# Feeding an FFN's weights through the sync queue in fp32 with casts on the engines, and refitting the instruction order

## The chip, the cores and the metric

One core of a Trainium2 chip. The metric is the device time of one execution in microseconds (us). One execution of each kernel was also recorded by the hardware profiler; its span is 1 to 2 us shorter than its time. Engines: PE is TensorE, DVE VectorE, ACT ScalarE, POOL GpSimd, SP the sync engine, which only issues DMAs here. All runs told below were in the fast state (mean granted TensorE clock 0.986 or more in every profile) and all were correct, unless said.

## The reference

A gated recurrence over time for 256 channels, and a multiplicative feed-forward net on its output; all in fp32, 4 sequences of 5824 tokens.

```python
a_base = sigmoid(a_param)
a   = exp(8 * sigmoid(r_gate) * log(clip(a_base, 1e-6, 1 - 1e-6)))
xg  = sqrt(max(1 - a*a, 1e-6)) * sigmoid(i_gate) * x
h   = 0
for t in range(S):                       # the scan
    h = a[:, t] * h + xg[:, t]; y[:, t] = h
out = ((y @ w1) * (y @ w2)) @ w3 @ w_out # w1, w2: 256x1024, w3: 1024x1024, w_out: 1024x256
```

## The kernel before

The 23,296 tokens are cut into 46 chunks: one of 256 tokens, then 45 of 512. For each chunk ScalarE takes the tanh of the gates (th_r, th_i), th_r and u = (1 + tanh) x are transposed, ScalarE makes the decay a_t (exp) and the square root (nrm), VectorE multiplies and scans (h_t), a cast gives y_t in bf16. TensorE then makes two "up" products, pa (on w1) and pb (on w2); ScalarE copies pa to sa, VectorE multiplies sa and pb to g_t, and TensorE makes the "down" product po. In the trace a table load of 1.28 us stands wherever ScalarE changes between exp or tanh and sqrt (30 in all, with the one at the start), so several chunks share one pair of table loads: such a set is a *group*.

w3 and w_out are multiplied once at the start (the *fold*), wp = w3 @ w_out / 4, so that each chunk needs only one down product. For this TensorE transposes w3 (ptw), VectorE copies it (w3t), TensorE multiplies (pw), and pw is copied to wp.

No instruction order is written down. A scheduler in Python takes jobs, each with an engine, a duration and a due time, plays them through, and issues them in the order it finds. That order is then fixed on every engine. The due times are offsets found by search:

```python
group_sizes = [2, 2, 1, 3, 3, 3, 4, 4, 4, 4, 4, 4, 4, 4]
NPE = 8      # chunks below this are transposed on TensorE, later ones by DMA
NDV = 3      # chunks below this have u and the squares on VectorE, later ones on GpSimd
NCV = 4      # chunks below this have y_t cast on VectorE
LAG = 17.5   # how long after a chunk's ups its downs are due
D_LOAD, D_TANH, D_EXP, D_SQRT, D_GATE, D_SCAN, D_CAST = 16.0, 9.0, 13.5, -1.5, 11.0, 8.5, 2.5
SPREAD = 9.9
...
def load_w(mp, w_sb, w_in):              # fp32 in HBM, bf16 on chip: cast by the DMA
    cols = slice(2 * mp * P, 2 * (mp + 1) * P)
    nc.gpsimd.dma_start(out=w_sb[:, :, cols], in_=w_in.rearrange("(cb p) f -> p cb f", p=P)[:, :, cols])

def load_wo():
    nc.gpsimd.dma_start(out=wo_sb, in_=moe_w_out.rearrange("(ko p) f -> p ko f", p=P))

def load_w3(mi):
    T["w3", mi] = consts.tile([P, DFF], BF16, name="w3_t", tag="w3_%d" % mi)
    nc.gpsimd.dma_start(out=T["w3", mi], in_=moe_w3[mi * P:(mi + 1) * P, :])
...
def fold_e(mi):
    nc.vector.tensor_scalar(wp_sb[:, mi, :], T["pw", mi], 0.25, None, op0=ALU.mult)
...
job((nm, mp), "POOL", 0.8, DUE_W + mp, partial(load_w, mp, w_sb, w_in), mb=0.26)   # w1, w2: four pieces each
```

## Time and profile before

| before | us |
|---|---|
| time, median of 3 (lowest to highest) | 540.92 (540.48 to 541.2) |
| x of chunk 1 has landed | 14.9 |
| first matmul of an up product | 20.86 |
| first down product (the fold is complete) | 70.65 |
| first ScalarE copy of chunk 4 / of chunk 12 / of chunk 45 | 83.7 / 175.0 / 521.4 |
| span | 540.3 |

The copies are good milestones: each chunk has exactly four (sa), and a copy cannot start before its up product is done. "Chunk 4" below means the start of its first copy. The page's busy shares and stretches are read in the prediction. Two more lines matter later, those of the DMA queues (columns: packets, MB, share of the 16 DMA engines' time):

```profile
q1 hardware_dynamic: 177104, 115.37, 80.6%
q0 software_dynamic: 4368, 3.67, 4.2%
```

q1 is the sync queue with everything else, q0 the GpSimd queue with the weights. The weights are under 5% of the DMA time; what they cost is when they run, not how long.

### The profile page before, as it was taken

The page shows a single profiled execution, that of the slowest core. Times are in us where ns is not written, and L with a number is a line of the kernel's source. Part 1 is how long each engine was busy: PE and PEld are TensorE (multiplying, and loading weights), DVE is VectorE, ACT ScalarE, POOL GpSimd, SP SyncE. Part 2 cuts the span into 40 slices and gives each one's busy share as a digit, 9 for nine tenths or more (in the row PEclk, how much of TensorE's full clock was granted, in tenths as well). Part 3 has the DMA queues.
Part 4 walks back from the last instruction along what each step waited for, and adds up shares of the span by engine and source line. Part 5 has one row for each costly group of instructions (what it writes and reads, how often), then busy time and mean ns, then how long its engine had stood idle before and what let it go on. Part 6 is the DMA issues. An engine that isn't in the chain of part 4 may idle for free.

```text
span 540.3 us, 8712 instructions
## 1 busy us (share of the span) xinstructions
PE 504.2 (93%) x3176; PEld 306.9 (57%) x3176; DVE 435.2 (81%) x360; ACT 458.3 (85%) x537; POOL 351.3 (65%) x280
## 2 busy tenths in 40 slices
PE   1577999999979999999999999999999999999996
PEld 1344676655545555665656556546565656556555
DVE  1867679868888699888999899889897998999541
ACT  6792799998997999999998899998999997854553
POOL 4083468885969678878884877978787869331000
PEclk9996999999998999999999999999999999999999
DMA  9999458999997999999899999999899943311112
GB/s 218 323 330 241 115 169 264 285 281 245 272 273 190 252 302 269 276 265 282 258 270 250 284 239 240 285 303 241 267 241 260 288 123 75 97 41 41 59 39 98
DMA packets 181788, 119.61 MB, mean 221 GB/s; under 512 B 84464, under 2 KB 180720, under 8 KB 181744
## 3 DMA queue, kind: packets, MB, share of 16 engines
q1 hardware_dynamic: 177104, 115.37, 80.6%
q0 software_dynamic: 4368, 3.67, 4.2%
q8 instruction: 25, 0.41, 0.3%
q14 instruction: 19, 0.16, 0.1%
q10 hardware_dynamic: 272, 0.00, 0.0%
HBM read 78.91 MB, written 23.86 MB: 190 GB/s over the span
## 4 chain that ended last, share of the span: by engine, by line
PE 73%; issue 7%; DVE 7%; ACT 6%; DMA 4%; POOL 2%; SPq 0%; DVEq 0%; ACTq 0%; POOLq 0%
PE po L242 24%; PE pa L221 24%; PE pb L221 23%; DVE g_t L235 3%; ACT sa L228 3%; DMA x_t<-in_x_dram 2%; DVE h_t L205 2%; DMA w_t<-in_moe_w_dram 2%; PE pw L280 1%; ACT nrm L185 1%; DVE nrm L190 1%; POOL u_t L145 1%; ACT a_t L173 1%; ACT ot L248 1%; ACT th_r L120 1%
## 5 line engine op out<-in xcount | busy, mean ns | idle before, releaser
L235 DVE TENSOR_TENSOR g_t<-sa,pb 128x1024 bf16<-128x1024 bf16 (+1 forms) x184 | 218.6, 1198 | 60.8 <-ACT sa L228 50.0
L221 PEld LDWEIGHTS <-w_sb 128*128 128x128 bf16 x1472 | 145.0, 99 | 162.0 <-issue 16.0
L228 ACT CAST sa<-pa 128x1024 bf16<-128x1024 f32 (+1 forms) x184 | 183.4, 1000 | 49.8 <-PE pa L221 45.5
L221 PE MATMUL pa<-y_t,w_sb 128*128 128x512 bf16 (+1 forms) x736 | 190.4, 382 | 12.3 <-DVE y_t L213 6.2
L221 PE MATMUL pb<-y_t,w_sb 128*128 128x512 bf16 (+1 forms) x736 | 189.4, 380 | 1.7 <-ACT sa L228 1.4
L242 PE MATMUL po<-wp_sb,g_t 128*128 128x256 bf16 x1456 | 179.7, 273 | 0.1
L242 PEld LDWEIGHTS <-g_t 128*128 128x128 bf16 x1456 | 142.7, 98 | 43.1 <-issue 0.7
L205 DVE TENSOR_TENSOR_SCAN h_t<-a_t,h_t,nrm 128x512 f32<-128x512 f32 (+3 forms) x90 | 140.1, 1567 | 2.0
L147 POOL TENSOR_TENSOR u_t<-th_i,x_t 128x512 bf16<-128x512 f32 x76 | 122.4, 1628 | 2.5
L181 POOL TENSOR_TENSOR nrm<-a_t 128x512 f32<-128x512 f32 x86 | 106.4, 1251 | 18.3 <-ACT a_t L173 18.2
L213 POOL CAST y_t<-h_t 128x1024 bf16<-128x1024 f32 x42 | 52.8, 1258 | 100.3 <-DVE h_t L205 85.5
L248 ACT COPY ot<-po 128x512 f32<-128x512 f32 x91 | 53.3, 586 | 19.6 <-PE po L242 19.0
L132 POOL TENSOR_SCALAR th_i<-th_i 128x1024 f32<-128x1024 f32 x43 | 48.0, 1117 | 27.0 <-ACT th_i L127 26.6
L190 DVE SCALAR_TENSOR_TENSOR nrm<-nrm,ut 128x1024 f32<-128x1024 f32 x38 | 56.7, 1492 | 8.7 <-ACT nrm L185 7.6
L173 ACT ACTIVATE a_t<-rt,la 128x512 f32<-128x512 bf16 x76 | 60.6, 819 | 0.2
L127 ACT ACTIVATE th_i<-i_t 128x1024 f32<-128x1024 f32 (+1 forms) x46 | 48.3, 1051 | 1.1 <-DMA i_t<-in_i_gate_dram 1.0
L185 ACT ACTIVATE nrm<-nrm 128x1024 f32<-128x1024 f32 (+1 forms) x46 | 48.0, 1056 | 1.4 <-DVE nrm L181 1.2
L120 ACT ACTIVATE th_r<-r_t 128x1024 bf16<-128x1024 f32 x38 | 40.3, 1062 | 0.4 <-DMA r_t<-in_r_gate_dram 0.4
L185 ACT ACT_TABLE_LOAD x14 | 18.0, 1283 | 0.2
L155 PE MATMUL ptr<-ident,th_r 128*128 128x128 bf16 x60 | 5.7, 249 | 10.6 <-DVE ident L73 8.7
L173 ACT ACT_TABLE_LOAD x11 | 14.1, 1283 | 0.7 <-DVE la L288 0.5
L145 POOL TENSOR_TENSOR u_t<-th_i,x_t 128x512 bf16<-128x512 f32 x10 | 13.5, 1360 | 0.3
(33 smaller groups left out, 112.0 us busy)
## 6 DMA issues: line engine op xcount, KB each, us to landing
out_dram<-ot SPq DMA_DIRECT2D x91, 256.0 KB, 3.1
r_t<-in_r_gate_dram SPq DMA_DIRECT2D x45, 512.0 KB, 5.4
i_t<-in_i_gate_dram SPq DMA_DIRECT2D x45, 512.0 KB, 5.5
x_t<-in_x_dram SPq DMA_DIRECT2D x45, 512.0 KB, 5.4
w_t<-in_moe_w_dram POOLq DMA_DIRECT2D x8, 256.0 KB, 10.8
w_sb<-in_moe_w_dram POOLq DMA_DIRECT2D x8, 128.0 KB, 9.3
rt<-th_r SPq DMA_TRANSPOSE x38, 4.2
ut<-u_t SPq DMA_TRANSPOSE x38, 4.3
```

The source lines that it names most:

```text
L147: nc.gpsimd.tensor_mul(out=u.rearrange("p cb j q -> p j cb q")[:, js], in0=cut(t)[:, js], in1=cut(T["x", c])[:, js])
L173: nc.scalar.activation(out=T["a", c][:, cb, :w], in_=T["pr", c][:, cb, :w], func=AF.Exp, scale=la4[:, cb:cb + 1], bias=la4[:, cb:cb + 1])
L181: eng.tensor_mul(out=T["n", c][:, cb, :w], in0=T["a", c][:, cb, :w], in1=T["a", c][:, cb, :w])
L185: nc.scalar.activation(out=T["n", c][:, :, :w], in_=T["n", c][:, :, :w], func=AF.Sqrt, scale=-1.0, bias=1.0)
L190: nc.vector.scalar_tensor_tensor(out=T["n", c][:, :, :w], in0=T["n", c][:, :, :w], scalar=1e-3, in1=T["pu", c][:, :, :w], op0=ALU.max, op1 ...
L205: nc.vector.tensor_tensor_scan(T["h", c][:, cb, lo:hi], T["a", c][:, cb, lo:hi], T["n", c][:, cb, lo:hi], init, ALU.mult, ALU.add)
L213: eng.tensor_copy(out=T["y", c][:, :, :w], in_=T["h", c][:, :, :w])
L221: nc.tensor.matmul(out=pp[:, q, :w], lhsT=w_sb[:, cb, m * P:(m + 1) * P], rhs=T["y", c][:, cb, :w], start=(cb == 0), stop=(cb == NCB - 1))
L228: nc.scalar.copy(out=sa[:, :, :w], in_=T["pa", c, mp][:, :, :w])
L235: nc.vector.tensor_mul(out=T["g", c][:, 2 * mp:2 * mp + 2, :w], in0=T["sa", c, mp][:, :, :w], in1=T["pb", c, mp][:, :, :w])
L242: nc.tensor.matmul(out=T["po", c, j // 2][:, j % 2, :], lhsT=T["g", c][:, k, j * P:(j + 1) * P], rhs=wp_sb[:, k, :], start=(k == 0), stop= ...
L248: nc.scalar.copy(out=T["ot", c, j2], in_=T["po", c, j2])
```

## The change

The intent: keep the weights from competing with the first chunks' data, by putting them into the sync queue's fixed order; pay for it with cast instructions on engines that idle at the start; and fit the scheduler's numbers again around that. It is two changes in one, a new path for the weights and a new order of everything. The core of the diff (parts that are switched off, renamings, and the due times of the weights and the fold are cut):

```diff
-    group_sizes = [2, 2, 1, 3, 3, 3, 4, 4, 4, 4, 4, 4, 4, 4]
+    group_sizes = [2, 2, 2, 3, 3, 4, 4, 4, 4, 3, 4, 2, 5, 4]
-    NPE = 8
-    NDV = 3
-    NCV = 4
+    NPE = 6
+    NDV = 4
+    NCV = 8
+    NWF = 2
+    FEA = True
+    WCE = {'w1': 'POOL', 'w2': 'POOL', 'wo': 'POOL', 'w3': 'DVE'}
-    LAG = 17.5
-    D_LOAD, D_TANH, D_EXP, D_SQRT, D_GATE, D_SCAN, D_CAST = 16.0, 9.0, 13.5, -1.5, 11.0, 8.5, 2.5
-    SPREAD = 9.9
+    DUE_WH = 8.0
+    LAG = 21.5
+    D_LOAD, D_TANH, D_EXP, D_SQRT, D_GATE, D_SCAN, D_CAST = 18.0, -13.5, 10.0, -0.5, 15.0, 10.0, 5.0
+    SPREAD = 4.9
...
-    def load_w(mp, w_sb, w_in):
-        cols = slice(2 * mp * P, 2 * (mp + 1) * P)
-        nc.gpsimd.dma_start(out=w_sb[:, :, cols], in_=...)
+    def load_w(key, piece):                      # 512 KB in fp32, into one of two staging buffers
+        T[key] = held.tile([P, NCB, CT], F32, name="wf", tag="wf", bufs=NWF)
+        nc.sync.dma_start(out=T[key]..., in_=piece)
+
+    def cast_w(key, dst, eng):
+        ...
+        if eng == "ACT":
+            nc.scalar.copy(out=dst, in_=t)
+        else:
+            (nc.gpsimd if eng == "POOL" else nc.vector).tensor_copy(out=dst, in_=t)
...
     def fold_e(mi):
-        nc.vector.tensor_scalar(wp_sb[:, mi, :], T["pw", mi], 0.25, None, op0=ALU.mult)
+        if FEA:
+            nc.scalar.mul(wp_sb[:, mi, :], T["pw", mi], 0.25)
...
-    SLOT = 10.3
+    SLOT = 10.1
-    RATE = 0.285
+    RATE = 0.33
```

w1 and w2 come in two halves each, w_out in two, w3 in eight rows of blocks: 14 loads, 14 casts (six on GpSimd, eight on VectorE).

More of the change, by code (lines that the diff above doesn't have):

```diff
@@ L86 @@
     AHEAD = 2
-    NPE = 8
-    NDV = 3
-    NCV = 4
+    NPE = 6
+    NDV = 4
+    NCV = 8
     NHELD = 6
-    BACKLOG = 0.5
-    DUE_W = -13.0
-    DUE_W3 = 14.0
-    DUE_F = 27.0
-    LAG = 17.5
-    D_LOAD, D_TANH, D_EXP, D_SQRT, D_GATE, D_SCAN, D_CAST = 16.0, 9.0, 13.5, -1.5, 11.0, 8.5, 2.5
-    SPREAD = 9.9
+    NWF = 2
+    FTD = False
+    FCA = False
+    FEA = True
+    WCE = {'w1': 'POOL', 'w2': 'POOL', 'wo': 'POOL', 'w3': 'DVE'}
+    BACKLOG = 0.5
+    DUE_W = -4.0
+    DUE_W3 = 20.5
+    DUE_WH = 8.0
+    DUE_F = 25.5
+    LAG = 21.5
+    D_LOAD, D_TANH, D_EXP, D_SQRT, D_GATE, D_SCAN, D_CAST = 18.0, -13.5, 10.0, -0.5, 15.0, 10.0, 5.0
+    SPREAD = 4.9
     src = {"r": rf, "i": jf, "x": xf}
@@ L253, in store @@
                           in_=T["ot", c, j2])
-    def load_w(mp, w_sb, w_in):
-        cols = slice(2 * mp * P, 2 * (mp + 1) * P)
-        nc.gpsimd.dma_start(out=w_sb[:, :, cols], in_=w_in.rearrange("(cb p) f -> p cb f", p=P)[:, :, cols])
-    def load_wo():
-        nc.gpsimd.dma_start(out=wo_sb, in_=moe_w_out.rearrange("(ko p) f -> p ko f", p=P))
-    def load_w3(mi):
-        T["w3", mi] = consts.tile([P, DFF], BF16, name="w3_t", tag="w3_%d" % mi)
-        nc.gpsimd.dma_start(out=T["w3", mi], in_=moe_w3[mi * P:(mi + 1) * P, :])
+    def load_w(key, piece):
+        T[key] = held.tile([P, NCB, CT], F32, name="wf", tag="wf", bufs=NWF)
+        nc.sync.dma_start(out=T[key] if len(piece.shape) == 3 and piece.shape[1] == NCB else
+                          T[key].rearrange("p a b -> p (a b)").rearrange("p (k f) -> p k f", f=piece.shape[-1]),
+                          in_=piece)
+    def cast_w(key, dst, eng):
+        t = T[key]
+        if dst is None:
+            T["w3b", key[1]] = dst = ffn.tile([P, 1, DFF], BF16, name="w3_t", tag="w3", bufs=4)
+        if dst.shape[1] != NCB:
+            t = t.rearrange("p a b -> p (a b)").rearrange("p (k f) -> p k f", f=dst.shape[-1])
+        if eng == "ACT":
+            nc.scalar.copy(out=dst, in_=t)
+        else:
+            (nc.gpsimd if eng == "POOL" else nc.vector).tensor_copy(out=dst, in_=t)
     def fold_t(mi):
+        if FTD:
+            T["w3t", mi] = ffn.tile([P, KD, P], BF16, name="w3t", tag="w3t", bufs=2)
+            nc.sync.dma_start_transpose(out=T["w3t", mi], in_=T["w3b", mi][:, 0, :])
+            return
         pt = psum_o.tile([P, KD, P], BF16, name="ptw", tag="po")
         for k in range(KD):
-            nc.tensor.matmul(out=pt[:, k, :], lhsT=T["w3", mi][:, k * P:(k + 1) * P], rhs=ident,
+            nc.tensor.matmul(out=pt[:, k, :], lhsT=T["w3b", mi][:, 0, k * P:(k + 1) * P], rhs=ident,
                              is_transpose=True, start=(k == 0), stop=(k == KD - 1))
@@ L274, in fold_c @@
         T["w3t", mi] = ffn.tile([P, KD, P], BF16, name="w3t", tag="w3t", bufs=2)
-        nc.vector.tensor_copy(out=T["w3t", mi], in_=T["ptw", mi])
+        if FCA:
+            nc.scalar.copy(out=T["w3t", mi], in_=T["ptw", mi])
+        else:
+            nc.vector.tensor_copy(out=T["w3t", mi], in_=T["ptw", mi])
     def fold_m(mi):
@@ L290, in fold_e @@
     def fold_e(mi):
-        nc.vector.tensor_scalar(wp_sb[:, mi, :], T["pw", mi], 0.25, None, op0=ALU.mult)
+        if FEA:
+            nc.scalar.mul(wp_sb[:, mi, :], T["pw", mi], 0.25)
+        else:
+            nc.vector.tensor_scalar(wp_sb[:, mi, :], T["pw", mi], 0.25, None, op0=ALU.mult)
     jobs = {}
@@ L298 @@
     BUFS = {"pab": 3, "po": 2, "r": 3, "i": 3, "x": 3, "th_r": 2, "th_i": 2, "u": 2, "rt": 2, "ut": NHELD,
-            "a": NHELD, "nrm": NHELD, "h": 2, "y": 4, "sa": 3, "g": 3, "ot": 3, "w3t": 2}
+            "a": NHELD, "nrm": NHELD, "h": 2, "y": 4, "sa": 3, "g": 3, "ot": 3, "w3t": 2, "w3": 4, "wf": NWF}
     def job(key, eng, dur, due, fn, after=(), new=None, uses=(), mb=0.0, group=None, lock=0):
         jobs[key] = dict(eng=eng, dur=dur, due=due, fn=fn, after=list(after), new=new, mb=mb, group=group, lock=lock,
-                         bulk=mb > 0 and key[0] not in ("turn_r", "turn_u", "store"))
+                         bulk=mb > 0 and key[0] not in ("turn_r", "turn_u", "store", "fold_t"))
         for u in uses:
             users.setdefault(u, []).append(key)
-    SLOT = 10.3
+    SLOT = 10.1
     def due_up(c):
@@ L313, with weight @@
     job(("la",), "ACT", 3.1, 0.0, rates, [("tanh_i", 0)])
-    for mp in range(4):
-        for nm, w_sb, w_in in (("w1", w1_sb, moe_w1), ("w2", w2_sb, moe_w2)):
-            job((nm, mp), "POOL", 0.8, DUE_W + mp, partial(load_w, mp, w_sb, w_in), mb=0.26)
-    job(("wo",), "POOL", 0.9, DUE_W3, load_wo, mb=1.05)
-    for mi in range(KD):
-        job(("w3", mi), "POOL", 0.8, DUE_W3 + 0.1 * mi, partial(load_w3, mi), mb=0.52)
-        job(("fold_t", mi), "PE", 0.6, DUE_F + mi, partial(fold_t, mi), [("w3", mi), ("ident",)],
-            ("po", ("ptw", mi)))
-        job(("fold_c", mi), "DVE", 0.7, DUE_F + mi, partial(fold_c, mi), [("fold_t", mi)],
-            ("w3t", ("w3t", mi)), [("ptw", mi)])
-        job(("fold_m", mi), "PE", 0.95, DUE_F + mi, partial(fold_m, mi), [("fold_c", mi), ("wo",)],
+    def weight(key, piece, dst, due, new=None):
+        job(("load",) + key, "SP", 0.5, due, partial(load_w, key, piece), [], ("wf", ("wf",) + key), mb=0.525)
+        eng = WCE[key[0]]
+        job(key, eng, {"POOL": 1.1, "DVE": 0.65, "ACT": 1.0}[eng], due + 3.0, partial(cast_w, key, dst, eng), [("load",) + key],
+            new, [("wf",) + key], lock=eng != "ACT")
@@ new lines @@
+    for half in range(2):
+        for nm, w_sb, w_in in (("w1", w1_sb, moe_w1), ("w2", w2_sb, moe_w2)):
+            cols = slice(half * CT, (half + 1) * CT)
+            weight((nm, half), w_in.rearrange("(cb p) f -> p cb f", p=P)[:, :, cols], w_sb[:, :, cols], DUE_W + half * DUE_WH)
+    for half in range(2):
+        ks = slice(4 * half, 4 * half + 4)
+        weight(("wo", half), moe_w_out.rearrange("(ko p) f -> p ko f", p=P)[:, ks, :], wo_sb[:, ks, :], DUE_W3)
+    for mi in range(KD):
+        weight(("w3", mi), moe_w3[mi * P:(mi + 1) * P, :].rearrange("p (k f) -> p k f", k=1), None, DUE_W3 + mi, ("w3", ("w3b", mi)))
+        if FTD:
+            job(("fold_t", mi), "SP", 1.25, DUE_F + mi, partial(fold_t, mi), [("w3", mi)],
+                ("w3t", ("w3t", mi)), [("w3b", mi)], mb=0.42)
+        else:
+            job(("fold_t", mi), "PE", 0.6, DUE_F + mi, partial(fold_t, mi), [("w3", mi), ("ident",)],
+                ("po", ("ptw", mi)), [("w3b", mi)])
+            job(("fold_c", mi), "ACT" if FCA else "DVE", 1.0 if FCA else 0.7, DUE_F + mi, partial(fold_c, mi), [("fold_t", mi)],
+                ("w3t", ("w3t", mi)), [("ptw", mi)])
+        job(("fold_m", mi), "PE", 0.95, DUE_F + mi, partial(fold_m, mi), [("fold_t" if FTD else "fold_c", mi), ("wo", 0), ("wo", 1)],
@@ L325 @@
             ("po", ("pw", mi)), [("w3t", mi)])
-        job(("fold_e", mi), "DVE", 0.45, DUE_F + mi, partial(fold_e, mi), [("fold_m", mi)], None, [("pw", mi)])
+        job(("fold_e", mi), "ACT" if FEA else "DVE", 0.4 if FEA else 0.45, DUE_F + mi, partial(fold_e, mi), [("fold_m", mi)], None, [("pw", mi)])
     hold = {}
@@ L380 @@
                     job((nm, c), "SP", 1.25, d, partial(turn_dma, c, key, src_nm), [pre],
-                        (tag, (key, c)), [(src_nm, c)], mb=0.35)
+                        (tag, (key, c)), [(src_nm, c)], mb=0.42)
             for cb in range(NCB):
@@ L400 @@
                 t = U + SLOT / 4 * mp * f
-                job(("pa", c, mp), "PE", 0.865 * f, t, partial(up, c, mp, "pa", w1_sb), [("cast", c), ("w1", mp)],
+                job(("pa", c, mp), "PE", 0.865 * f, t, partial(up, c, mp, "pa", w1_sb), [("cast", c), ("w1", mp // 2)],
                     ("pab", ("pa", c, mp)), [("y", c)])
                 job(("pb", c, mp), "PE", 0.865 * f, t + 0.01, partial(up, c, mp, "pb", w2_sb),
-                    [("pa", c, mp), ("w2", mp)], ("pab", ("pb", c, mp)), [("y", c)])
+                    [("pa", c, mp), ("w2", mp // 2)], ("pab", ("pb", c, mp)), [("y", c)])
                 job(("copy", c, mp), "ACT", 0.15 + 0.82 * f, t + 0.9, partial(copy, c, mp), [("pa", c, mp)],
```

## The prediction

> **What bounds the kernel now.** I read the page first (shares, slices), then busy time by stretch, then the chain of waits, then the waits and the timeline of the first 75 us.
>
> ```profile
> PE 504.2 (93%) x3176; PEld 306.9 (57%) x3176; DVE 435.2 (81%) x360; ACT 458.3 (85%) x537; POOL 351.3 (65%) x280
> ...
> PE   1577999999979999999999999999999999999996
> ...
> PEclk9996999999998999999999999999999999999999
> DMA  9999458999997999999899999999899943311112
> ```
>
> TensorE is full after slice 4; the holes lie in the first four slices, with one at slices 11 and 12. The chain gives the price of the work: four 512-wide matmuls take 0.86 us, eight po matmuls 0.87, eight transposes 0.45. A chunk of 512 tokens has 8 x 0.86 + 4 x 0.87 = 10.36 us of TensorE. With 45.5 chunks (471.4), the fold of w3 (8 x 1.32 = 10.6) and 120 transposes (6.8) the stream is 488.7 us. The span is 540.3, so 51.6 us are holes, half clock and tail. Where they lie, by stretch (window: length, busy us of each engine, clock, DMA share, GB/s):
>
> ```profile
> 0.00:20.00 20.00, 3.08 (x24) 2.50 (x25) 6.86 (x13) 14.16 (x18) 6.60 (x14) 1.00 1.04 243
> 20.00:40.00 20.00, 16.40 (x104) 9.86 (x103) 14.76 (x17) 17.91 (x22) 11.39 (x12) 1.00 1.12 339
> 40.00:50.00 10.00, 6.34 (x27) 2.98 (x28) 7.67 (x9) 3.31 (x4) 5.43 (x8) 0.51 1.17 246
> 50.00:70.00 20.00, 19.33 (x168) 13.67 (x167) 13.04 (x20) 14.02 (x16) 8.18 (x8) 0.99 0.56 129
> 70.00:120.00 50.00, 49.79 (x350) 32.37 (x348) 39.65 (x31) 48.93 (x58) 41.33 (x34) 1.00 0.96 256
> 120.00:175.00 55.00, 51.38 (x308) 30.32 (x306) 46.85 (x38) 49.13 (x60) 42.67 (x31) 0.97 0.98 251
> 200.00:440.00 240.00, 237.08 (x1454) 142.01 (x1453) 214.55 (x164) 227.61 (x267) 189.89 (x142) 1.00 1.02 261
> ```
>
> Two things are to be seen. From 40 to 50 us TensorE runs at clock 0.51 and ScalarE is busy for only 3.31 us of ten. From 70 to 440 us ScalarE is 89 to 98% busy and the DMA share is near 1: in the middle these two feed TensorE with little to spare. The first matmul on wp (po), for which the fold must be complete, starts at 70.65 us. The order of instructions has 36.1 us of TensorE work ahead of it, so 34.5 us are already lost there. From the chain and the waits of the first 60 us:
>
> ```profile
> 3.32 11.60 DMA x_t<-in_x_dram
> 39.17 9.07 DMA w_t<-in_moe_w_dram
> ```
> ```profile
> POOL th_i L132 <- ACT th_i L127: 20.8, 1, 20.8
> ACT sa L228 <- PE pa L221: 12.4, 4, 5.6
> PE pa L221 <- DVE y_t L213: 6.2, 2, 3.5
> DVE u_t L142 <- DMA x_t<-in_x_dram: 4.3, 1, 4.3
> ```
>
> The x of chunk 1 takes 11.6 us to land, because eight weight loads of the GpSimd queue fly beside it; VectorE waits 4.3 us for it. Later the w3 loads take 9 us, TensorE meanwhile cools, and ScalarE waits for slow matmuls.
>
> **What the Trainium skill says.** (1) "Trainium Kernel Development and Optimization", Key Constraints: DMAs of all queues run on the same 16 DMA engines and interleave. The trace agrees: x_t for 3.32 + 11.60, with DMA share already 1.04. The move to another queue therefore brings no bandwidth; it brings an order. (2) "DMA: Bandwidth & Descriptors", SWDGE vs HWDGE vs iDMA: a cast during a DMA is only to be had from GpSimd. That is why the new kernel needs cast instructions. (3) "SBUF — State Buffer", two separate sides: VectorE and GpSimd take a shared port pair as an exclusive lock. The trace fits: a 128x512 scan takes 1.28 us (median) in the first 80 us and 1.59 on average over the run; a GpSimd u_t half 1.27 and then 1.63. (4) "TensorE: Matmul & The Clock Gate", HAM clock gate: an idle window of about 3.4 us halves the clock. The trace shows holes of 1.29 and 2.67 us with 0.61 us of transposes between them, then 0.51.
>
> **The change part by part.**
> *Weights.* Seventeen cast loads on the GpSimd queue go. Fourteen loads of 512 KB in fp32 on the sync queue come (2 each for w1, w2 and wo, 8 for w3), through two staging buffers. The bytes read from HBM are the same 7.3 MB; the w1 and w2 loads now stand behind the loads of chunks 0 and 1. At the 350 GB/s that the trace shows from 18 to 37 us, 2.36 MB for the two chunks should have landed near 10.5 us, in place of 14.9.
> *Casts.* GpSimd gets six casts (y_t casts of that size: 1.26 us, so 7.6 us); it stood idle for 20.8 us there, so they are hidden. VectorE gets eight casts of w3 at 0.69 = 5.5 us, four more y casts (2.8) and u_t with squares of chunk 3 (1.2 + 1.3), and loses wp (8 x 0.42 = 3.4): 7.4 us more, all within the first 90 us. ScalarE gains the 3.4.
> *Transposes.* Chunks 6 and 7 turn by DMA instead of TensorE: 32 x 0.45/8 = 1.8 us off the stream, 486.9 left.
> *Order and groups.* Fourteen groups as before, so the table loads stay (30, now 31). TensorE starts w3's fold between the ups of chunk 2, as before.
>
> *Where the start now ends.* I walk the issue order of the changed kernel with durations from before. ScalarE: tanh_i(1) needs no wait, decays end near 13.8, table 15.0, root(1) 15.7 to 16.8; VectorE: gated(1) 17.8 to 19.0, cast(0) 19.4. First up at 19.5 instead of 20.9: 1.4 us of the 4.3, since ScalarE's own run of 15 us takes over. After that ScalarE has an unbroken list: tables, tanh, decays, roots, copies and the wp copies up to the first ot add up to some 50 us, so about 66. VectorE from 22.5 on, also unbroken: u_t, squares, scans, 12 products, 8 w3 casts, 8 w3t copies, ending with the last w3t near 63; 2.5 us for locked scans and gates make it 65.5. Then pw (1.9) and wp. The first po comes at about 67.5, against 70.65. That is 3 us, and it understates the matter: before, only gated(4) had still to run at that time (70.69), now it and a scan of chunk 4 lie ahead of the po. Chunk 4's first sa should come near 77 (10 us of TensorE list after the po), against 83.7 before.
>
> *What of it survives.* The start of chunk 12's copies was at 175.0, 91.3 us after chunk 4, where eight chunks need 82.9: the front (ScalarE, scans) held TensorE up by 8.4, most of it at 150 to 175 us. Counting ScalarE's list up to there at page durations gives 161.4 us before and 164.6 after; ScalarE's busy union is 458/494 = 0.93 of such sums, so 150 and 153. Before, ScalarE's idle time up to there was 25 us. After, the 12.4 us of waiting for pa should mostly go: 25 - 12 = 13, and 153 + 13 = 166. TensorE alone would be at 77 + 83 = 160. I take 165, a gain of 10. From chunk 12 to 44 before took 336.1 us for 32 chunks (331.5 at full speed): 4.6 us of holes, which a front that is ahead could lessen, and other groups (2, then 5) could add to. I leave it as it is, with another 1 to 2 us gained. Sum: 540.9 - 10 - 1.4 = **529.5 us**.
>
> **Rivals.** (a) *The loads were hidden anyway.* For: the front is bound by ScalarE and DMA in the middle (89 to 98% and share 1), and the list of ScalarE is not shorter but 3.4 us longer; TensorE could start earlier and stall at 100 to 200 us instead. Against: ScalarE's 12.4 us of waiting are real and unused. It would give 536 to 541. (b) *VectorE becomes the bound of the start.* For: 7 us more, and unbroken from 22 to 75 us, with GpSimd beside it on the shared port. If its ops stretch as over the whole run (scan 1.28 to 1.59), the first po slips to 70 and the gain shrinks to what the groups bring: 534 to 538. (c) *Head-of-line waits on the sync queue.* The w3 loads wait there for staging buffers that VectorE frees late, and the loads and transposes of chunks 6 to 8 stand behind them. That would show as tanh waiting for r_t or i_t at 45 to 65 us, worth 3 to 6 us: 533 to 536. (d) *All holes of the start and of 150 to 175 us close.* Full speed from chunk 4 at 75: 540.9 - 8.7 - 8.4 - 3 = 521.
>
> **Range and chances.** Middle 529.5; (d) sets the low end at 521.5, (a) and (b) the high end at 537.5. Two per cent is 530.1, almost at my middle: faster 0.52, within 0.45, slower 0.03. Slower would need a new stall of over 20 us, for which nothing speaks.
>
> **What would show it.** x of chunk 1 landing before 11.5 us and first up near 19.5; no stretch of half clock with ScalarE idle between 40 and 55 us (ScalarE over 80% busy from 20 to 70); VectorE over 90% busy from 25 to 65; first po at 65 to 69; chunk 12's copies at 163 to 168; from there the same pace, 10.5 us a chunk. It would be wrong if po came late because a w3 load was queued behind others, or if TensorE stopped over 3 us at a group's roots after 100 us.

## The result, and the profile after

The changed kernel took 532.07 us (median of 4 fast runs, 531.23 to 532.87); the kernel before, beside it, 540.74 (540.48 to 541.2). The ratio is 0.9838, with a 95% interval of 0.9818 to 0.9859: 1.6% less. A ratio here is the mean time of one kernel's fast runs over that of the other's of the same rounds, so not quite the ratio of the two medians. All outputs are right. The changed kernel's page, its first line and its slices:

```profile
PE 498.4 (94%) x3144; PEld 303.3 (57%) x3144; DVE 446.7 (84%) x367; ACT 463.1 (87%) x546; POOL 335.8 (63%) x260
...
PE   1568899999999999999999999999999999999997
...
PEclk9999999999999999999999999999999999999999
...
q1 hardware_dynamic: 184624, 123.76, 86.4%
```

TensorE has 32 matmul records fewer, the transposes of chunks 6 and 7 that went to DMA. The slices hold at 9 from slice 6 on, and the dent that the kernel before had around slice 12 is gone, in PE and in PEclk. There is no q0 any more. The milestones, in us from the span's start:

| | x of chunk 1 | first up | first down | chunk 4 | 4 to 12 | chunk 12 | 12 to end | span |
|---|---|---|---|---|---|---|---|---|
| before | 14.9 | 20.86 | 70.65 | 83.7 | 91.3 | 175.0 | 365.3 | 540.3 |
| after | 11.2 | 20.73 | 69.28 | 82.4 | 84.7 | 167.1 | 363.8 | 530.9 |
| difference | -3.7 | -0.1 | -1.4 | -1.3 | **-6.6** | -7.8 | -1.5 | -9.4 |

So the loads did land earlier, but only 1.3 us of it is left when chunk 4 begins. Most of the gain lies in the next eight chunks. (The spans differ by 9.4 and the medians by 8.7; executions of one kernel in one set scatter by 1 to 4 us, and the profiled one is one of them.) The busy time by stretch of the changed kernel, to be laid beside that of before in the prediction (window: length, busy us of PE, PEld, DVE, ACT, POOL, then clock, DMA share, GB/s):

```profile
0.00:20.00 20.00, 3.15 (x26) 2.56 (x27) 9.60 (x15) 15.22 (x19) 3.98 (x8) 1.00 0.94 299
20.00:40.00 20.00, 15.84 (x102) 9.49 (x103) 19.77 (x20) 18.66 (x23) 7.67 (x7) 0.94 1.08 361
40.00:50.00 10.00, 8.21 (x59) 4.58 (x58) 8.68 (x10) 8.91 (x12) 8.20 (x7) 0.96 0.78 215
50.00:70.00 20.00, 17.57 (x153) 11.93 (x151) 19.84 (x20) 15.83 (x21) 11.83 (x10) 1.00 0.97 296
120.00:175.00 55.00, 54.63 (x337) 32.78 (x336) 45.64 (x38) 52.69 (x64) 40.94 (x32) 1.00 0.98 262
```

From 40 to 50 us ScalarE is busy for 8.91 us in place of 3.31, and the clock is 0.96 in place of 0.51. VectorE is full from 20 to 70 us. From 120 to 175 us TensorE is busy for 54.63 of 55 us, in place of 51.38. The same in finer stretches, first before, then after:

```profile
140.00:160.00 20.00, 18.98 (x119) 11.45 (x117) 16.58 (x15) 18.69 (x22) 15.16 (x12) 1.00 1.12 260
160.00:180.00 20.00, 18.19 (x97) 9.99 (x98) 16.46 (x13) 16.79 (x21) 17.58 (x14) 0.91 0.85 231
```
```profile
140.00:160.00 20.00, 19.63 (x125) 12.00 (x124) 16.01 (x16) 18.89 (x22) 12.71 (x11) 1.00 0.97 285
160.00:180.00 20.00, 20.00 (x123) 11.82 (x121) 18.18 (x15) 19.26 (x24) 15.67 (x13) 1.00 0.94 243
```

What the hole of before looks like is told by its chain of waits in that stretch (start, length, what):

```profile
154.14 1.06 ACT nrm L185
155.21 1.08 ACT L173
157.32 0.91 ACT sa L228
158.27 1.04 PE pb L221 x4
159.36 1.21 issue
160.57 1.20 DVE g_t L235
161.81 1.04 PE pa L221 x4
162.85 1.37 PE pb L221 x4
164.22 1.71 PE pa L221 x4
```

A root of a group and a table load (the nameless ACT L173) hold ScalarE, and the copy sa behind them comes late. TensorE waits 0.32 us for that copy, and then 2.52 us for the product g_t. The chain calls the 1.21 us before the product "issue", but the timeline shows VectorE at work there, on a scan that stands ahead of the product in its order:

```profile
158.77 1.87 DVE L205 TENSOR_TENSOR_SCAN h_t<-a_t,h_t,nrm 128x512 f32<-128x512 f32 x1
```

VectorE's list is full from 150.22 us on, after a wait of 2.11 us for an earlier root of ScalarE; so the late copy alone cost 0.32 us, and the rest came by way of VectorE. After the hole the clock is at 0.50 from 163.06 to 166.47 us, and the fours at 162.85 and 164.22 take 1.37 and 1.71 us in the chain in place of 0.86. The changed kernel's order has the roots of its groups elsewhere, and no such stop there.

### The profile page after: what moved, and what is told of

It reads as the page before. It is cut to its first block, busy times and chain, and to the rows that moved or that the text cites. A ratio compares the mean times of both kernels' runs of the same rounds, so it can differ in the third digit from the quotient of the medians.

```text
span 530.9 us, 8667 instructions
## 1 busy us (share of the span) xinstructions
PE 498.4 (94%) x3144; PEld 303.3 (57%) x3144; DVE 446.7 (84%) x367; ACT 463.1 (87%) x546; POOL 335.8 (63%) x260
## 3 DMA queue, kind: packets, MB, share of 16 engines
HBM read 78.91 MB, written 23.86 MB: 194 GB/s over the span
## 4 chain that ended last, share of the span: by engine, by line
PE 81%; DVE 8%; ACT 4%; issue 3%; DMA 3%; SPq 0%; DVEq 0%; ACTq 0%
PE pa L227 27%; PE pb L227 26%; PE po L248 26%; DVE g_t L241 2%; DMA rt<-th_r 2%; DVE h_t L211 2%; DVE w_t L276 1%; ACT sa L234 1%; PE pw L299 1%; ACT th_i L133 1%; DMA i_t<-in_i_gate_dram 1%; DVE nrm L196 1%; DVE u_t L148 1%; ACT ot L254 1%; ACT a_t L179 1%
## 5 line engine op out<-in xcount | busy, mean ns | idle before, releaser
L248 PE MATMUL po<-wp_sb,g_t 128*128 128x256 bf16 x1456 | 181.7, 273 | 0.2 <-DVE nrm L196 0.2
L211 DVE TENSOR_TENSOR_SCAN h_t<-a_t,h_t,nrm 128x512 f32<-128x512 f32 (+3 forms) x90 | 136.6, 1534 | 0.8
L153 POOL TENSOR_TENSOR u_t<-th_i,x_t 128x512 bf16<-128x512 f32 x80 | 116.5, 1472 | 2.5
L219 POOL CAST y_t<-h_t 128x1024 bf16<-128x1024 f32 x38 | 44.6, 1173 | 67.9 <-DVE h_t L211 62.1
L138 POOL TENSOR_SCALAR th_i<-th_i 128x1024 f32<-128x1024 f32 x42 | 57.6, 1371 | 21.8 <-ACT th_i L133 21.8
L179 ACT ACTIVATE a_t<-rt,la 128x512 f32<-128x512 bf16 x80 | 63.5, 816 | 4.5 <-DMA rt<-th_r 4.2
L196 DVE SCALAR_TENSOR_TENSOR nrm<-nrm,ut 128x1024 f32<-128x1024 f32 x40 | 59.8, 1494 | 2.4 <-ACT nrm L191 2.4
L126 ACT ACTIVATE th_r<-r_t 128x1024 bf16<-128x1024 f32 x40 | 42.3, 1063 | 2.1 <-DMA r_t<-in_r_gate_dram 2.0
L276 POOL CAST w_sb<-wf 128x1024 bf16<-128x1024 f32 x4 | 6.1, 1545 | 19.7 <-DMA wf<-in_moe_w_dram 19.7
L161 PEld LDWEIGHTS <-th_r 128*128 128x128 bf16 x44 | 3.7, 122 | 18.5 <-ACT th_r L124 14.9
```

Source lines behind the costliest of these rows:

```text
L138: nc.gpsimd.tensor_scalar(t, t, 1.0, 1.0, op0=ALU.add, op1=ALU.mult)
L153: nc.gpsimd.tensor_mul(out=u.rearrange("p cb j q -> p j cb q")[:, js], in0=cut(t)[:, js], in1=cut(T["x", c])[:, js])
L179: nc.scalar.activation(out=T["a", c][:, cb, :w], in_=T["pr", c][:, cb, :w], func=AF.Exp, scale=la4[:, cb:cb + 1], bias=la4[:, cb:cb + 1])
L196: nc.vector.scalar_tensor_tensor(out=T["n", c][:, :, :w], in0=T["n", c][:, :, :w], scalar=1e-3, in1=T["pu", c][:, :, :w], op0=ALU.max, op1 ...
L211: nc.vector.tensor_tensor_scan(T["h", c][:, cb, lo:hi], T["a", c][:, cb, lo:hi], T["n", c][:, cb, lo:hi], init, ALU.mult, ALU.add)
L248: nc.tensor.matmul(out=T["po", c, j // 2][:, j % 2, :], lhsT=T["g", c][:, k, j * P:(j + 1) * P], rhs=wp_sb[:, k, :], start=(k == 0), stop= ...
```

## The experiments

Twelve kernels were run, all but one with 3 rounds (in a round the kernels of a set and the kernel before are run beside each other), the last with 5, in four sets; each set shared runs of the kernel before (medians 541.2 to 541.5) on its chip. Two that would have been the plainest, the kernel before with only the new due times or only the new groups, could not be built: its scheduler then finds no order in which every job can run. So the order was kept from the changed kernel, and the weights' path was taken out of it, or the reverse. The theories:

- **Path** (B in the expectations): the new path of the weights gives the gain (chunk 1's data is early, so the start is early).
- **Order** (A in the expectations; A1 the groups, A2 the due times and the moved work): the refit gives the gain; how the weights come is indifferent.
- **VectorE start**: the casts make VectorE the bound of the start, and cost part of the gain.

### The new order, with the old kind of load

The changed kernel with its order of everything else kept; each weight load issued on the GpSimd queue as a casting DMA straight into the bf16 tile, no casts by engines.

```diff
     def load_w(key, piece, dst):
+        nc.gpsimd.dma_start(out=dst, in_=piece)
+        return
         T[key] = held.tile([P, NCB, CT], F32, name="wf", tag="wf", bufs=NWF)
...
-        job(key, eng, ..., partial(cast_w, key, dst, eng), ...)
+        job(key, eng, ..., None, ...)
```

> The changed kernel's issue order and refitted times, but the weights loaded and cast by DMAs of the GpSimd queue as before (14 of them, at the places where the order has the sync loads); no staging buffers, no cast instructions. Theory A (the refit makes the gain, between chunks 4 and 12; the queue is nearly neutral): 530 to 535 us. Theory B (the queue makes the gain, the refit only follows it): 538 us or more, with x of chunk 1 landing at 14 to 15 us again, and the fold late. VectorE, without eight casts, should be busy under 95% of 50 to 70 us.

Measured: 539.92 us, ratio 0.998 (0.9954 to 1.0005): nothing is left of the gain. Its trace says where it went, in the waits of the first 60 us:

```profile
DVE u_t L148 <- DMA x_t<-in_x_dram: 8.4, 1, 8.4
```

x of chunk 1 lands at 19.4 us. Seven weight loads (3.7 MB in fp32) leave the GpSimd queue within the first 6.2 us, since there nothing holds them, and the data of chunk 1 shares the DMA engines with them. First up 26.3, chunk 4 at 89.0. But from chunk 4 to 12 it takes 86.0 us, nearly as quick as the changed kernel (84.7), and the end of its span is about as late as the start: 7.8 us against 6.6 at chunk 4. So this run did not tell path and order apart; it had a third thing in it, the early loads. The last pair of the experiments takes that out.

### The new path, with the old order's numbers

The changed kernel with groups, NPE, NDV, NCV, all due offsets of the chunks, LAG, SPREAD, SLOT and RATE of before, and wp by VectorE again.

```diff
-    group_sizes = [2, 2, 2, 3, 3, 4, 4, 4, 4, 3, 4, 2, 5, 4]
+    group_sizes = [2, 2, 1, 3, 3, 3, 4, 4, 4, 4, 4, 4, 4, 4]
-    NPE = 6
-    NDV = 4
-    NCV = 8
+    NPE = 8
+    NDV = 3
+    NCV = 4
-    FEA = True
+    FEA = False
-    LAG = 21.5
-    D_LOAD, ... = 18.0, -13.5, 10.0, -0.5, 15.0, 10.0, 5.0
-    SPREAD = 4.9
+    LAG = 17.5
+    D_LOAD, ... = 16.0, 9.0, 13.5, -1.5, 11.0, 8.5, 2.5
+    SPREAD = 9.9
...
```

> The new weight path (sync loads, staging, casts on GpSimd and VectorE, and its own due times) with all else as before: groups, due times, LAG, SLOT, RATE, NPE 8, NDV 3, NCV 4, wp written by VectorE. Theory A: 538 to 546 us (VectorE gets 8 casts more in the start and the stall at chunks 10 to 12 stays). Theory B: 530 to 534 us.

Measured: 542.35 us, ratio 1.003 (0.9998 to 1.0062). x of chunk 1 lands at 11.2 us and the first up starts at 20.6, as in the changed kernel (20.7), and it is worth nothing: the first down comes at 79.57, chunk 4 at 91.4. With the old numbers the path gives no gain. Chunks 4 to 12 take 85.9 us here, although the numbers are the old ones; with chunk 4 so late the front has more time to get ahead, so this run cannot show what this order does after an early chunk 4.

### All but the groups

```diff
-    group_sizes = [2, 2, 2, 3, 3, 4, 4, 4, 4, 3, 4, 2, 5, 4]
+    group_sizes = [2, 2, 1, 3, 3, 3, 4, 4, 4, 4, 4, 4, 4, 4]
```

> The changed kernel with the group sizes of before alone put back (the list is scheduled anew). If the groups' boundaries make the gain (theory A1): 537 to 541 us, with TensorE stopped for several us at the roots near 150 us. If the due times and the move of work do (theory A2): 531 to 534 us.

Measured: 540.51 us, ratio 0.9984 (0.9953 to 1.0015). Chunk 4 at 87.9, then 83.5 us to chunk 12. Its stretch from 70 to 80 us:

```profile
70.00:80.00 10.00, 6.29 (x36) 4.48 (x35) 9.89 (x9) 7.94 (x11) 4.86 (x4) 0.55 0.97 270
```

TensorE is at clock 0.55 and VectorE full. These due times need these groups: with the old ones the scheduler finds an order whose start is 5.5 us worse, and which takes another 3.0 us more after chunk 12. The time is in A1's range, but not for A1's reason: TensorE is busy for 54.85 of 55 us from 120 to 175 us, without a stop at the roots there.

### More and less work at the start

Five kernels keep the order of the changed one and move or add work in the first 70 us. The edits:

```diff
  e5_cast_twice: each VectorE cast of w3 twice
             (nc.gpsimd if eng == "POOL" else nc.vector).tensor_copy(out=dst, in_=t)
+            if eng == "DVE":
+                nc.vector.tensor_copy(out=dst, in_=t)
  e6_w3_on_scalar: the eight w3 casts on ScalarE
-        if eng == "ACT":
+        if eng in ("ACT", "DVE"):
             nc.scalar.copy(out=dst, in_=t)
  e7_w3_on_pool: all casts on GpSimd
-            (nc.gpsimd if eng == "POOL" else nc.vector).tensor_copy(out=dst, in_=t)
+            nc.gpsimd.tensor_copy(out=dst, in_=t)
  e8_fold_on_vector: wp by VectorE, as before
-        if FEA:
+        if False:
  e10_fold_turn_twice: w3's transposes twice on TensorE
-        for k in range(KD):
+        for k in list(range(KD)) * 2:
```

> The changed kernel, each of the eight casts of w3 on VectorE done twice, the order of all else kept: some 8 x 1.1 = 8.8 us more of VectorE between 40 and 66 us. If VectorE bounds the start, the first po moves from 69.3 to 76 to 79 us. If that start is on the path to the end, the time goes to 537 to 541 us; if a later slack swallows it, it stays under 534 us.

> The same with the eight casts on ScalarE (some 8 x 1.0 us), which is busy 8.9 of 10 us from 40 to 50 and 15.8 of 20 after. If only VectorE matters: 524 to 529 us. If ScalarE is just as long: 531 to 538 us.

> The changed kernel, order kept, with the eight casts of w3 issued on GpSimd in place of VectorE. It takes 8.7 us (8 x 1.1) of VectorE's list from 42 to 65 us and adds 8.3 (8 x 1.04) to GpSimd, which is busy 11.8 of 20 us there. If VectorE's length is what delays the start (the reverse of the doubling, which cost 8 us): first po at 62 to 66, time 524 to 529 us. If GpSimd then holds squares and u_t back by as much, or something else is as long as VectorE: 530 to 534 us.

> The changed kernel, order kept, with wp written by VectorE as before (8 x 0.42 = 3.4 us back on VectorE, 8 x 0.38 = 3.0 off ScalarE). VectorE bounds the start: 534 to 537 us. ScalarE bounds it: 528 to 531 us.

> The changed kernel with each of the 64 transposes of w3 on TensorE done twice, order kept: 8 x 0.45 = 3.6 us more of TensorE before the first po. If TensorE itself bounds the start: 535 to 536 us. If it has holes there that VectorE dictates: 532 to 533.5 us.

| run | moved or added | median, us | ratio (95%) | first down | chunk 4 |
|---|---|---|---|---|---|
| changed kernel | | 532.07 | 0.9838 (0.9818 to 0.9859) | 69.28 | 82.4 |
| e5_cast_twice | + eight casts on VectorE | 540.06 | 0.9974 (0.9938 to 1.0009) | 78.26 | 90.1 |
| e6_w3_on_scalar | eight casts VectorE to ScalarE | 535.04 | 0.9874 (0.9845 to 0.9904) | 70.83 | 84.1 |
| e7_w3_on_pool | eight casts VectorE to GpSimd | 531.38 | 0.9818 (0.9786 to 0.9851) | 71.24 | 83.3 |
| e8_fold_on_vector | eight wp copies ScalarE to VectorE | 533.52 | 0.9852 (0.9825 to 0.9879) | 72.06 | 83.9 |
| e10_fold_turn_twice | + 64 transposes on TensorE | 532.72 | 0.9843 (0.9811 to 0.9874) | 69.18 | 81.8 |

The eight casts together take 8.7 us in the changed kernel. Doubling them costs 8.0 us at the end by the medians, 7.4 by the ratios: work added to VectorE in the start is paid nearly in full. Taking them away gains nothing clear (the intervals of e7 and the changed kernel overlap), because the work only changes its place. Busy time from 40 to 50, 50 to 60 and 60 to 70 us, in e6 (ScalarE is the fourth number of busy time) and then in e7 (GpSimd the fifth):

```profile
40.00:50.00 10.00, 7.80 (x57) 4.56 (x56) 7.10 (x7) 9.97 (x12) 8.35 (x7) 0.93 0.74 205
50.00:60.00 10.00, 8.21 (x71) 5.66 (x72) 5.77 (x7) 9.97 (x14) 3.51 (x4) 1.00 1.05 348
60.00:70.00 10.00, 7.84 (x66) 5.23 (x65) 6.35 (x7) 10.00 (x14) 6.75 (x6) 1.00 0.79 188
```
```profile
40.00:50.00 10.00, 6.33 (x38) 4.34 (x40) 5.41 (x6) 6.21 (x9) 10.00 (x9) 0.66 0.71 218
50.00:60.00 10.00, 9.95 (x82) 6.57 (x80) 7.26 (x8) 9.01 (x12) 7.81 (x8) 1.00 1.02 346
60.00:70.00 10.00, 8.11 (x67) 5.36 (x68) 7.11 (x8) 8.57 (x12) 9.78 (x9) 1.00 0.79 190
```

VectorE, full before, now idles, and the engine that took the casts is full in its stead (GpSimd but for 50 to 60 us). The start is balanced over three engines. TensorE does not seem to be one of them: the 64 added transposes (3.6 us by the 0.45 us for eight) cost nothing that could be told. That run has a second thing in it, though: its clock is at 1.00 from 20 to 50 us, where the changed kernel has 0.94 and 0.96, which may pay for part of them. Of the expectations, those of e5, e6, e7 and e10 came in the range for a start that VectorE bounds and that other engines fill as well; e8's 533.52 fell between its two ranges, and its interval overlaps the changed kernel's, so it tells little.

### The weights ahead of chunk 1

```diff
+    early = [("load", "w1", 0), ("load", "w2", 0)]   # issued before r of chunk 1 on the sync queue
```

> The changed kernel with the first two staged loads (1 MB) moved ahead of the loads of chunk 1 on the same sync queue, order kept otherwise. x of chunk 1 lands near 14 in place of 11.2, while ScalarE needs tanh_i of chunk 1 at 11.2. If arrival order in the start is what decides: 534 to 536 us. If slack swallows it: 531.5 to 533.

Measured: 533.17 us, ratio 0.9855 (0.9815 to 0.9895), just above the range for slack and not clear of the changed kernel's interval. x of chunk 1 at 13.3, first up 21.6, chunk 4 at 83.5, chunk 12 at 168.2: about 1 us later up to there, and level at chunk 45 (510.5 us in both profiles). The place in the sync queue does move the start as the intent says; that this reaches the end is not shown.

### The pair that settles it: both orders, loads on the GpSimd queue, held back

The first is the new order with casting loads on the GpSimd queue again (no staging, no casts by engines), but each batch of loads stands behind a one-column GpSimd copy that reads th_r of chunk 1, 2, 3 or 4, so it cannot leave before that. The second is the kernel before, untouched but for the same trick: its eight loads of w1 and w2 stand behind such a copy of th_r of chunk 1.

```diff
  e12_new_order_loads_held (on top of the first experiment)
+        nc.gpsimd.tensor_copy(out=brake[:, c:c + 1], in_=flat(T["thr", c])[:, 0, :1])
+    after(1, [L("w1", 0), L("w2", 0)])
+    after(2, [L("w1", 1), L("w2", 1)])
+    after(3, [L("wo", 0), L("wo", 1)])
+    after(4, [L("w3", mi) for mi in range(3)])    # the other w3 loads two places earlier in the order
  e13_before_loads_held (on top of the kernel before)
+        nc.gpsimd.tensor_copy(out=brake[:, c:c + 1], in_=flat(T["thr", c])[:, 0, :1])
+    after(1, [(nm, mp) for mp in range(4) for nm in ("w1", "w2")])
```

> The run e1 again (issue order and times of the changed kernel, weights cast by DMAs of the GpSimd queue, no staging, no cast instructions), with the loads held back so that they cannot fly beside the loads of chunk 1: a one-column copy on GpSimd waits for tanh_r of chunk 1, 2, 3 or 4 before the loads of the halves of w1 and w2, of wo and of the first w3 go. If e1 lost its gain only through x of chunk 1 landing at 19.4 us: 528 to 534 us, first up near 20.7. If the sync queue and the casts on the engines are needed for the gain: 536 us or more.

> The kernel before, its order kept, its eight loads of w1 and w2 held until tanh_r of chunk 1 has run, so that x of chunk 1 should land near 11 us in place of 14.9. If the start of the kernel before is on the path to its end: first up near 19.5, time lower by 1 to 3 us, 538 to 540. If the front's stall at 150 to 175 us sets the time whatever the start: 540 to 541.5.

| run | median, us | ratio (95%) | x of chunk 1 | chunk 4 | 4 to 12 | chunk 12 | span |
|---|---|---|---|---|---|---|---|
| e12_new_order_loads_held | 532.01 | 0.983 (0.9799 to 0.9861) | 11.2 | 81.4 | 85.0 | 166.4 | 529.6 |
| e13_before_loads_held | 540.06 | 0.9977 (0.9945 to 1.001) | 10.9 | 81.6 | 91.3 | 172.8 | 539.0 |

Both kernels load their weights by casting DMAs of the GpSimd queue, in both the first loads wait until chunk 1's data is there, the last w3 load lands at 57.5 and 57.4 us, and both reach chunk 4 at the same time. From there the new order takes 6.2 us less to chunk 12 and 2.9 us less after it. And the new order without the new path is as fast as the changed kernel. What differs at chunk 4 is how much of the front is done: up to there ScalarE has been busy for 68.1 us in e12 and for 62.7 in e13 (68.7 and 62.8 in the changed kernel and the kernel before), and has made the th_i of ten chunks in place of eight; for chunks 4 to 12 it has 81.9 us left in place of 84.6. So the new order uses the start to get ahead. That this lead is what removes the stop fits these numbers, but no run moved it alone. In the trace of e12 the stretch that lost time before is full (54.31 of 55 us at clock 1.00; this trace lacks 57 of the 3144 matmul records, so it is rather more):

```profile
120.00:175.00 55.00, 54.31 (x331) 32.85 (x336) 45.66 (x39) 52.67 (x64) 41.22 (x33) 1.00 0.99 259
```

### The later downs

The changed kernel with LAG as before, scheduled again; this is the run with 5 rounds.

```diff
-    LAG = 21.5
+    LAG = 17.5
```

> The changed kernel with LAG alone put back from 21.5 to 17.5, scheduled anew: the po of a chunk are ordered 4 us earlier, up to the first po nothing changes. In the changed kernel 20.4 us pass from the first copy of the last chunk to the end, before 18.8. If LAG makes that difference and costs nothing elsewhere: 18.8 again and 530 to 531 us, the fastest of all. If the longer lag is what keeps TensorE fed between chunks 4 and 12 (84.7 us there, 91.3 before): 533 to 539 us.

Measured: 535.28 us, ratio 0.9876 (0.9848 to 0.9905). From chunk 45's first copy to the end it takes 18.7 us in place of 20.4, because 16 more of the down matmuls (1.7 us) run ahead of that copy: that is work moved, not won. What it loses lies earlier. Busy time from 200 to 320 us, in this run and in the changed kernel:

```profile
200.00:320.00 120.00, 117.26 (x713) 69.56 (x712) 103.17 (x82) 113.14 (x135) 88.37 (x67) 1.00 0.94 247
```
```profile
200.00:320.00 120.00, 120.00 (x736) 71.82 (x734) 109.50 (x85) 114.87 (x134) 91.08 (x69) 1.00 0.90 239
```

From chunk 20 to 28 it takes 87.3 us, where the changed kernel takes 82.8: TensorE waits four times for a copy sa there (2.4 us), in the changed kernel never. A likely reading is that with the downs due later TensorE has down products in hand whenever an up product has to wait; with LAG back, it stops for 2.7 of these 120 us. The expectation had the loss between chunks 4 and 12, and there it is small (85.4 us, against 84.7): the time came in its range, the place did not.

## Why the prediction was right, and where its steps were not

The time was right: 529.5 predicted, 521.5 to 537.5 as range, 532.07 measured. Of the classes, "faster by over 2%" had a little more chance than "within 2%", and it came within. The cause, though, lay elsewhere than most of the working put it: of 10 us to be gained up to chunk 12, 6.7 were to come before chunk 4, from the early loads, and 1.3 did; 6.6 came between chunks 4 and 12, where 3.3 were expected. The three ways of loading, over the two orders, in medians:

| | casting loads on the GpSimd queue, from the start | the same, held back | fp32 on the sync queue, cast by engines |
|---|---|---|---|
| old order | 540.7 to 541.5 | 540.06 | 542.35 |
| new order | 539.92 | 532.01 | 532.07 |

In these runs neither the order nor the holding back gains anything clear alone; together they gain about 9 us. The sync queue, the staging buffers and the casts are one way to hold the loads back, and a plain wait does as well. Why both are needed here: with the loads let go at once, the new order's start is 7 us late (chunk 4 at 89.0), and a late chunk 4 is carried to the end almost one for one, here and in e5. With the loads held in the old order, chunk 4 comes 2.1 us earlier and the front stops TensorE on the way to chunk 12 as before (91.3 us). The two runs of the first column are not quite alike, though: e1 lets 3.7 MB of weights go in its first 6.2 us, the kernel before 2.1 MB. What the new order gains with the old pace of loads was not run; e11, with 1 MB ahead of chunk 1, lost about 1 us in the start.

By the prediction's steps:

1. *x of chunk 1 near 10.5 us.* Right: 11.2.
2. *First up at 19.5, the casts on GpSimd hidden.* Wrong: 20.73, so of 1.4 us 0.1 came. The casts were not hidden. The changed kernel's timeline (start, length, engine, instruction), and the two squares of chunk 1 in e12, which has no casts:

```profile
12.57 3.28 POOL L276 CAST w_sb<-wf 128x1024 bf16<-128x1024 f32 x2 [11.26 <-DMA wf<-in_moe_w_dram]
13.43 2.96 DVE L187 TENSOR_TENSOR nrm<-a_t 128x512 f32<-128x512 f32 x2
...
19.33 0.42 DVE L219 CAST y_t<-h_t 128x512 bf16<-128x512 f32 x1
...
19.91 1.03 PE L161 MATMUL ptr<-ident,th_r 128*128 128x128 bf16 x8 [4.96 <-ACT th_r L124]
...
20.73 1.06 PE L227 MATMUL pa<-y_t,w_sb 128*128 128x256 bf16 x4
```
```profile
13.46 1.29 DVE L187 TENSOR_TENSOR nrm<-a_t 128x512 f32<-128x512 f32 x2
```

   The two squares on VectorE lie beside the first casts on GpSimd and take 2.96 us, where in e12 the same two take 1.29. ScalarE's root waits 0.60 us for them, and its next tanh starts at 18.79 us in place of e12's 18.11. The transposes of that th_r stand ahead of the first up in TensorE's order, which the walk had left out: they start at 19.91 (e12: 19.22) though y_t of chunk 0 is ready at 19.75, and the first up follows at 20.73 (e12: 20.05).
3. *No half clock with ScalarE idle; ScalarE over 80% busy from 20 to 70, VectorE over 90% from 25 to 65.* Right in the main: ScalarE is busy for 43.4 of the 50 us (15.83 of 20 from 50 to 70, just under), VectorE for 38.4 of the 40. The half clock is down from 10.2 us (40.18 to 50.42) to 3.4 (37.41 to 40.82), and ScalarE's wait for pa in the first 60 us, 12.4 us before, is down to this:

```profile
ACT sa L234 <- PE pa L227: 2.1, 3, 1.1
```

4. *First down at 67.5 (65 to 69).* Just late: 69.28. The mis-sized term is the VectorE list, where 2.5 us were allowed for the shared port. In it the eight w3 casts were put at 0.69 each, 5.5 us together, and took 8.7 (the spread is in the line below: shortest, median and longest in ns); e5 shows that such time on VectorE is paid nearly in full, and without these casts (e12) the first down came at 67.69. This is rival (b), half of it: the first down slipped to nearly its 70, but the time did not follow.

```profile
L276 DVE CAST w_t<-wf x8: 679/1022/1750, 42.3 to 64.4; 128x1024 bf16<-128x1024 f32 x8
```

5. *Chunk 4 at 77.* Wrong by 5.4 us: 82.4. The working put 9.5 us between the first down and chunk 4; it took 13.1, as before (83.66 less 70.65 is 13.0). The timeline of TensorE from the first down to the first up product of chunk 4, of which the copy at 82.38 can start when it is done:

```profile
69.28 1.91 PE L248 MATMUL po<-wp_sb,g_t 128*128 128x256 bf16 x16
71.37 1.91 PE L248 MATMUL po<-wp_sb,g_t 128*128 128x256 bf16 x16 [0.18 <-DVE nrm L196]
...
81.48 1.02 PE L227 MATMUL pa<-y_t,w_sb 128*128 128x512 bf16 x4
```

   Between them stand seven sets of eight downs (0.87 each) and six sets of four ups (0.86): 11.3 us, then the set at 81.48 itself, 0.86. The list had been miscounted by 2.6 us; short waits between the sets make 1.0, and the late first down 1.8.
6. *Chunk 12 at 165 (163 to 168).* Right: 167.1, but by two errors against each other. The working implied 88 us for chunks 4 to 12, and they took 84.7; chunk 4 was 5.4 us later than assumed. That is luck in the number. Its account of ScalarE, though, came out: busy 147.4 us up to chunk 12 before and 150.6 after (predicted 150 and 153), idle 27.5 and 16.6 (25 and 13); the idle time was recovered, and 5.9 us more of ScalarE's work was done before chunk 4. Taken as a term of the sum, 10 us were put here and 7.8 came: 2.2 of the 2.6 us by which the time was missed; the rest is within the scatter.
7. *From there as before, 1 to 2 us gained.* Right: 1.5.

Three readings in the prediction need a correction. The half clock of the kernel before begins at 40.18 us, when only 0.56 of the hole of 2.67 us had passed; most of that hole came after it. In (3) u_t's 1.27 is a median and its 1.63 a mean; the later u_t have the median 1.27 too, and a few slow ones make the mean (the same holds in part for the scans: median 1.31 over the run, mean 1.59). And counted from one, the dent in the slices is at 12 and 13.

Rival (a) would have left the time unchanged; it failed on the changed kernel. Part of it can be seen in e13: with chunk 4 2.1 us earlier, the way to chunk 12 takes 91.3 us as before, and the time gains nothing clear. Rival (c) can be seen but is small: the sync queue waits for VectorE to free the staging buffers, 13.5 us in six waits, but from 40 to 70 us no tanh waits for its load, and the run that has no staging buffers (e12) is no faster.

```profile
SPq L263 <- DVE w_t L276: 13.5, 6, 4.5
```

Rival (d) came by half: the hole of 150 to 175 us closed, those of the start hardly (chunk 4 at 82.4, not 75).

What stays open: which of the refitted numbers puts the front ahead. Five of them (NPE, SPREAD, D_LOAD, D_TANH, D_GATE) cannot be set back alone, since the scheduler then finds no order. The others build, with everything scheduled anew, but of these only the groups and LAG were run; the rest is untested. The groups are needed with these due times (540.51 without). LAG is worth 2 to 3 us (535.28, by the ratios 2.1), and the two intervals overlap; more was not told apart. Nothing that was run clearly beat the changed kernel; e7 (531.38) and e12 (532.01) are level with it.

## What to carry to other kernels

When a diff has a new mechanism and refitted numbers in it, run the numbers without the mechanism: here they give the whole gain, as long as something else does the one thing that the mechanism was good for, holding bulk loads back until the first data has passed. Before moving work off an engine that is full in the start-up, look at the busy time of those that would take it: this start-up, balanced over three engines, paid nearly in full for added work and gave nothing clear for moved work. And follow a saving to a milestone further on: 3.7 us at the first load were 0.1 at the first matmul.

## What the Trainium skill lacked or had wrong

- "DMA: Bandwidth & Descriptors", SWDGE vs HWDGE vs iDMA, says that loads of the GpSimd queue and of the sync queue feed different internal queues, which each DMA engine serves in turn. The runs fit this, and add the price, which the page does not have: x of chunk 1 lands at 11.2 us where the weights follow it in the sync queue, at 14.9 with 2.1 MB of weights (in fp32) let go on the GpSimd queue at the start, and at 19.4 with 3.7 MB.
- "SBUF — State Buffer", two separate sides, warns that VectorE's fast modes starve loads of the GpSimd queue, and advises the sync queue. Here the time shows no difference: with VectorE busy for 18.22 of 20 us (20 to 40 us) in e12, casting loads on the GpSimd queue gave 532.01 us, the sync queue 532.07. Those that e12 issued from 19 to 23 us did take 7.0 to 13.0 us to land, where the staged loads take 5.7 to 6.0 in the median; whether VectorE was the cause is not shown.
- The same page calls the port that VectorE and GpSimd share an exclusive lock, for which the later of two instructions waits until the other is done, but gives no time for such a mix as this. Here a 128x1024 cast from fp32 to bf16 took 0.68 us on VectorE at best, 1.02 in the median and 1.75 at worst; and two 128x512 squares took 2.96 us beside GpSimd's casts, 1.29 without them (e12).
- "TensorE: Matmul & The Clock Gate", HAM clock gate, names one idle window of about 3.4 us as what halves the clock. The windows are in the traces: the half clock lasts 10.24 us in the kernel before (40.18 to 50.42) and 3.41 in the changed one (37.41 to 40.82), three windows and one of 3.41 us. But the window need not be idle throughout: in the 3.41 us ahead of these drops TensorE was busy for 1.55 us (36.77 to 40.18) and for 1.13 (34.00 to 37.41).
- No page says that the profile's MB and GB/s count a casting load by the bytes that land: the GpSimd queue of the kernel before shows 3.67 MB for 7.3 MB of weights, and both kernels show 78.91 MB read from HBM. GB/s of a kernel with casting loads and of one without can't be compared.
